# First four pairs of heads eased off ScalarE, two more parts of GEMM 2 in seven products, and a new instruction order

## The chip, the cores and the metric

The kernel runs on one core of one Trainium2 chip. The metric is the device time in microseconds, as a median of several runs. Beside it stands one execution taken by the hardware profiler. Engines are named as the profile names them: PE is TensorE, DVE VectorE, ACT ScalarE, POOL GpSimd, SP the engine that issues the DMAs.

## The reference

Attention with random features over 64 heads, and a two-layer network on its output:

```python
batch, n_heads, seq, head_dim = (8, 8, 576, 64); n_features = 128
n_tokens, d_model, d_ff = (4608, 512, 2048)
def phi(x):
    proj = np.einsum('bhsd,md->bhsm', x, omega)
    sq = np.sum(x * x, axis=-1, keepdims=True) / 2.0
    h = proj - sq
    h = h - np.max(h, axis=-1, keepdims=True)
    return np.exp(h) / np.sqrt(m)
q_p, k_p = (phi(q_s), phi(k_s))
kv = np.einsum('bhsm,bhsd->bhmd', k_p, v)
z = np.sum(k_p, axis=2)
num = np.einsum('bhsm,bhmd->bhsd', q_p, kv)
den = np.einsum('bhsm,bhm->bhs', q_p, z)[..., None] + 1e-06
...
h = x @ w_in
sp = np.maximum(h, 0.0) + np.log1p(np.exp(-np.abs(h)))
g = h * erf(sp)
return g @ w_out
```

All of it is float32.

## The kernel before

**Pairs.** Heads are done two at a time, 32 pairs, named `b_p` (batch and pair): `uk`, `uq` hold the transposed k and q of a pair with their squares, `ppk`, `ppq` the projections in PSUM, `mxk`, `mxq` the negated row maxima, `fk`, `fq` the exponentials, `kvp` and its copy `kh` the product of k's features with v, `pt` the transposed `fq`, `qh` its copy out of PSUM, `nd` numerator and denominator, `rc` the reciprocal by Ln and Exp on ACT, `xs` the quotient. The first eight pairs square with `square`, on 64 partitions; the first four are done before the network begins.

**Supers.** The network goes over six blocks of tokens ("supers") of 2 x 288, 2 x 288 and four times 2 x 432. A float32 product is made of three in fp32r, of a rounded part and a rest (`xh`, `xl`; `gh`, `gl`). GEMM 1 gives `h` (supers 0 and 1) or `hX`, `hY`, `hZ` (supers 2 to 5, where seven block products stand for eight; `PRODUCTS`). GEMM 2 goes in four parts (quarters of d_ff) per super. `FIRST2` says from which super a part has seven products (`gemm2_blocks`: banks `oX`, `oY`, `oZ`, operands `bb`, `bh`, `th`, `bl`, `tl` from `pieces2`) and not eight (`gemm2`: bank `o`, operands `gh`, `gl`). `pieces2` forms four differences (`gs`) and rounds five operands. The sums of weights that the seven products need are made by `make_sums` in the super ahead of the first that uses them, and stored in DRAM (`wdc`). Super 2's input needs the pairs up to 3_3.

**Weights.** Each block of weights comes as 64-bit words and is put together once: shift (`st`, DVE), a ScalarE step and a join (`wt`), a rounding and a rest (`w`), in supers 0 and 1.

**Order.** `build` lists operations with the engines that may take them, a cost and the slack from which an engine takes them. `Plan.order` plays them with estimated costs, `LAG` between engines, slots and due times; a program is emitted in the order that it picks, and each engine runs its own in that order. All compute instructions are issued on line 1008 (1031 in the changed kernel), so the names of tiles tell them apart.

Of the kernel before, what the change touches and what calls it, by code (L numbers as in the profile page):

```python
# [19 lines left out]
P = 128  # L20
# [44 lines left out]

FIRST2 = (3, 3, 3, 3)

# [7 lines left out]
BANDWIDTH = 270e3  # L75
LAG = {"T": 0.35, "A": 0.25, "V": 0.25, "G": 0.3, "S": 0.3}
SLOTS = dict(w=8, g=11, u=2, f=2, mx=3, sq=3, v=1, qh=1, ql=1, kh=1, kl=1, xs=12, xh=2, xl=2,
# [28 lines left out]
class Plan:  # L106
# [43 lines left out]
    def order(self, slots, caps):  # L150
# [167 lines left out]

AHEAD = 40.0

# [25 lines left out]
SQN = 4  # L346
SQG = -1e9
SQA = 4.0
# [4 lines left out]
def build(emit):  # L353
# [162 lines left out]
    def load(n, qk):  # L516
# [28 lines left out]
        for i in range(parts):  # L545
            keys = range(3) if parts == 1 else [i]
            f = 1.0 / parts
            pl.op("sq" + qk, [("A", 1.17 * f + .1, -1e9)] if n == 0 else
                  [("G", 2.2, SQG if n < SQN else -1e9), ("A", 1.2, -1e9 if n < SQN else SQA)],
                  lambda e, i=i: E.square(e, u, qk, i, parts),  # L550
                  reads=[(u, ("x", c)) for c in keys], writes=[(u, ("s", c)) for c in keys])

    def project(n, qk, t0):
# [15 lines left out]
        else:  # L569
# [5 lines left out]
            order = range(3)  # L575
        less = (n, qk) in LESS
        for i in order:
# [4 lines left out]
        if rows:  # L582
# [3 lines left out]
                  reads=keys + [(sq, 0)], writes=keys[:1] + [(mx, k) for k in range(NC)])  # L586
        for i in order:
            c = chunks[i]
            if less:
                pl.op("less" + qk, [("V", 0.56, -1e9)], lambda e, i=i, c=c: E.less(f, mx, banks[i], c),  # L590
                      reads=[(banks[i], 0)] + [(mx, k) for k in c], writes=[(f, k) for k in c])
# [4 lines left out]
        if less:  # L596
            pl.op("exp" + qk, [("A", 1.16, -1e9)], lambda e: E.exponential_all(f),
                  reads=[(f, k) for k in range(NC)], writes=[(f, k) for k in range(NC)], set="exp")

    def key_values(n, t0):  # L600
# [7 lines left out]
        kl = a["kl"] = kh if whole else pl.tile("kl", "kl" + a["nm"], [P, 2, P], F32R)  # L608
        pl.op("kvhigh", [("V", 0.6, -1e9), ("A", 0.7, -1e9)], lambda e: E.kv_high(e, kh, kvp),
              reads=[(kvp, 0)], writes=[(kh, 0)])  # L610
# [4 lines left out]
    def turn(n, t0):  # L615
# [48 lines left out]
    def split(b, c):  # L664
# [326 lines left out]
def tile_attention_moe(ctx: ExitStack, tc: tile.TileContext, qT, kT, qR, kR, qN, kN, vP, omT, w1, w2, out):  # L991
# [68 lines left out]
    class Emit:  # L1060
# [111 lines left out]

# [197 lines left out]
```

## Time and profile before

| | us |
|---|---|
| median of 3 runs (1030.12 to 1030.81) | 1030.14 |
| the profiled execution | 1036.67 |
| its span, first to last instruction | 1034.9 |
| PE busy in it | 1006.5 |
| DVE, ACT, POOL busy | 795.1, 683.7, 628.5 |
| mean granted clock of TensorE | 0.993 |

Busy time of PE counts pipelined products from start to modelled end, so a product's own cost is read from the distance of starts, or from a run of them in the chain of waits.

### The profile page before, as it was taken

What the parts mean: (1) busy time and instruction counts of PE and PEld (TensorE: products, weight loads), DVE (VectorE), ACT (ScalarE), POOL (GpSimd) and SP (SyncE); (2) the same over time, 40 slices, a digit from 0 to 9 for tenths busy, and PEclk for the clock granted to TensorE, in tenths of its full rate; (3) what the DMA queues carried; (4) which work ended last, traced back from release to release, by engine and by line L of the source; (5) the groups of instructions that cost most, each with busy time, mean ns of one, the idle gap of its engine ahead of it and who ended that gap; (6) DMA issues with size and microseconds to landing.
All of it is one profiled execution on the core that took longest, in us unless ns stands there. A gap on an engine that the chain in (4) does not pass through costs nothing.

```text
span 1034.9 us, 19457 instructions
## 1 busy us (share of the span) xinstructions
PE 1006.5 (97%) x7132; PEld 932.1 (90%) x7132; DVE 795.1 (77%) x1288; ACT 683.7 (66%) x1285; POOL 628.5 (61%) x467
## 2 busy tenths in 40 slices
PE   7999999999999899999999999999999999999998
PEld 6899889988999699999989899989899999999997
DVE  4888978897877747657787786889887788778664
ACT  7879887785676656855757575767658565645550
POOL 3435544875677728636876847569765388687520
PEclk9999998999999999999999999999999999999999
DMA  8276777597777467766547876666687546686651
GB/s 218 83 239 221 277 270 249 191 365 278 252 246 240 149 233 242 237 229 220 189 163 252 286 247 222 224 227 221 215 278 236 192 166 220 225 291 220 229 183 69
DMA packets 99486, 232.72 MB, mean 225 GB/s; under 512 B 11200, under 2 KB 11712, under 8 KB 99392
## 3 DMA queue, kind: packets, MB, share of 16 engines
q1 hardware_dynamic: 99232, 231.42, 67.1%
q8 instruction: 57, 0.93, 0.4%
q14 instruction: 37, 0.30, 0.1%
q10 hardware_dynamic: 160, 0.07, 0.0%
HBM read 188.45 MB, written 42.99 MB: 224 GB/s over the span
## 4 chain that ended last, share of the span: by engine, by line
PE 83%; DVE 8%; ACT 4%; DMA 3%; issue 2%; SPq 1%; ACTq 0%; DVEq 0%
PE o L1008 16%; PE hX L1008 14%; PE oX L1008 9%; PE h L1008 8%; PE hY L1008 7%; PE nd L1008 6%; PE oY L1008 5%; PE ppq L1008 4%; PE hZ L1008 4%; PE kvp L1008 3%; PE ppk L1008 3%; PE oZ L1008 2%; PE pt L1008 2%; DMA w<-wdw 1%; ACT L1008 1%
## 5 line engine op out<-in xcount | busy, mean ns | idle before, releaser
L1008 PE MATMUL o<-gh,w 128*128 128x288 f32 (+1 forms) x832 | 211.1, 329 | 0.6 <-DVE w L1008 0.6
L1008 PE MATMUL hX<-xh,wb 128*128 128x432 f32 x512 | 166.1, 370 | 2.3 <-DVE hs L1008 1.3
L1008 POOL TENSOR_TENSOR hs<-gs,hs 128x864 f32<-128x864 f32 (+1 forms) x44 | 97.6, 2242 | 101.0 <-ACT gs L1008 93.7
L1008 PEld LDWEIGHTS o<-gh,w 128*128 128x128 f32 x832 | 144.6, 188 | 6.1 <-DVE w L1008 1.1
L1008 PE MATMUL o<-gl,w 128*128 128x288 f32 (+1 forms) x416 | 132.7, 319 | 0.1
L1008 PE MATMUL h<-xh,w 128*128 128x288 f32 x512 | 126.0, 317 | 4.4 <-DVE w L1008 1.8
L1008 PEld LDWEIGHTS hX<-xh,wb 128*128 128x128 f32 x512 | 96.2, 188 | 9.1 <-DVE hs L1008 1.9
L1008 ACT ACT_TABLE_LOAD x75 | 96.2, 1283 | 2.1 <-PEq L1361 0.7
L1008 PEld LDWEIGHTS h<-xh,w 128*128 128x128 f32 x512 | 88.4, 193 | 9.4 <-DVE w L1008 2.5
L1008 PE MATMUL hX<-xl,wb 128*128 128x432 f32 x256 | 91.6, 358 | 0.0
L1008 ACT ACTIVATE fq<-ppq,mxq 128x128 f32<-128x128 f32 x288 | 78.6, 388 | 16.7 <-DVE mxq L1008 16.0
L1008 ACT ACTIVATE fk<-ppk,mxk 128x128 f32<-128x128 f32 x288 | 82.2, 380 | 9.7 <-DVE mxk L1008 9.3
L1008 ACT ACTIVATE hs<-hX 128x432 f32<-128x432 f32 x70 | 37.3, 532 | 74.6 <-PE hX L1008 73.8
L1008 PE MATMUL nd<-qh,kh 128*128 128x288 f32 x256 | 79.6, 417 | 7.2 <-ACT qh L1008 2.7
L1008 PE MATMUL hY<-xh,wb 128*128 128x432 f32 x256 | 84.0, 369 | 0.0
L1008 PE MATMUL oX<-th,wb 128*128 128x432 f32 x264 | 83.8, 367 | 0.0
L1008 ACT ACTIVATE rc<-nd,eps 64x288 f32<-64x288 f32 x128 | 63.6, 497 | 29.1 <-PE nd L1008 25.9
L1008 PEld LDWEIGHTS o<-gl,w 128*128 128x128 f32 x416 | 78.3, 188 | 2.9 <-DVE gl L1008 0.4
L1008 POOL TENSOR_TENSOR uq<-uq 128x288 f32<-128x288 f32 (+1 forms) x46 | 39.9, 888 | 67.2 <-PE h L1008 15.0
L1008 PE MATMUL h<-xl,w 128*128 128x288 f32 x256 | 76.7, 300 | 0.0
L1008 POOL TENSOR_TENSOR uk<-uk 128x288 f32<-128x288 f32 (+1 forms) x52 | 44.9, 884 | 51.1 <-DMA uk<-kT 23.4
L1008 DVE TENSOR_TENSOR xs<-nd,rc 64x288 f32<-64x288 f32 (+1 forms) x160 | 62.9, 393 | 14.9 <-ACT rc L1008 11.7
(142 smaller groups left out, 2700.2 us busy)
## 6 DMA issues: line engine op xcount, KB each, us to landing
wb<-wdc SPq DMA_DIRECT2D x216, 256.0 KB, 3.5
wb<-wdw SPq DMA_DIRECT2D x162, 256.0 KB, 3.8
w<-wdw SPq DMA_DIRECT2D x52, 512.0 KB, 4.5
st<-w SPq DMA_DIRECT2D x32, 512.0 KB, 5.0
wdw<-w SPq DMA_DIRECT2D x32, 512.0 KB, 4.4
wdc<-c SPq DMA_DIRECT2D x32, 512.0 KB, 4.8
v<-vP SPq DMA_DIRECT2D x32, 325.0 KB, 4.6
uk<-kR SPq DMA_DIRECT2D x24, 320.0 KB, 3.7
```

Of the source, the lines that this page charges most:

```text
L1008: return tc.keep_in_program_order(method(*args, **kwargs))
```

## The change

1. `FIRST2` goes from (3, 3, 3, 3) to (3, 3, 2, 2): parts 3 and 4 of GEMM 2 have seven products from super 2 on, and their sums of weights are made in super 1.
2. In the first pairs some steps may no longer go to ACT: pair 0's squares of q go to DVE, those of pairs 1 to 3 to POOL or DVE; the copies of `kvp` and `pt` of pairs 0 to 3 go to DVE alone; the rounding of super 0's input goes to POOL or DVE.
3. The planner's lags and `AHEAD` have other values, and `JITTER` moves due times within 26 stretches by fixed amounts, so that the order differs almost everywhere.
4. The three projections into a bank now have one start and one stop flag. `LIFT` and `LESS` are empty lists: the code that they switch emits nothing.

```diff
-FIRST2 = (3, 3, 3, 3)
+FIRST2 = (3, 3, 2, 2)
-LAG = {"T": 0.35, "A": 0.25, "V": 0.25, "G": 0.3, "S": 0.3}
+LAG = {"T": 0.32375, "A": 0.2525, "V": 0.2605, "G": 0.2979, "S": 0.2925}
+        for k, (lo, hi, amp) in enumerate(JITTER):
+            for o in ops:
+                if lo <= o.due < hi:
+                    o.due += amp * ((o.id * 7919 + k * 104729 + 17) % 1009 / 504.0 - 1.0)
-AHEAD = 40.0
+JITTER = ((0, 0, 0), (186.1, 206.1, 4), (0, 0, 0), (0, 0, 0), (0, 0, 0), (227.5, 727.5, 4),
...
+AHEAD = 39.82
-SQG = -1e9
+SQV = 3.0
+EASED = 4
-            pl.op("sq" + qk, [("A", 1.17 * f + .1, -1e9)] if n == 0 else
-                  [("G", 2.2, SQG if n < SQN else -1e9), ("A", 1.2, -1e9 if n < SQN else SQA)],
+            pl.op("sq" + qk, [("A" if qk == "k" else "V", 1.17 * f + .1, -1e9)] if n == 0 else
+                  [("G", 2.2, -1e9), ("V", 1.27, SQV)] if n < SQN else [("G", 2.2, -1e9), ("A", 1.2, SQA)],
-        pl.op("kvhigh", [("V", 0.6, -1e9), ("A", 0.7, -1e9)], lambda e: E.kv_high(e, kh, kvp),
+        pl.op("kvhigh", [("V", 0.6, -1e9), ("A", 0.7, -1e9)][:1 + (n >= EASED)], lambda e: E.kv_high(e, kh, kvp),
-            pl.op("turnhigh", [("A", 0.5, -1e9), ("V", 0.5, -1e9)],
+            pl.op("turnhigh", [("V", 0.5, -1e9), ("A", 0.5, -1e9)][:1 + (n >= EASED)],
-            pl.op("xhigh", [("A", 0.2 + 0.24 * m, -1e9), ("G", 0.1 + 0.35 * m, 2.0),
-                            ("V", 0.1 + 0.18 * m, -1e9)],
+            pl.op("xhigh", [("A", 0.2 + 0.24 * m, -1e9)] * (b > 0) +
+                  [("G", 0.1 + 0.35 * m, 2.0), ("V", 0.1 + 0.18 * m, -1e9)],
+            elif e == "V":
+                dve.tensor_mul(u.ap[dst, c], u.ap[src, c], u.ap[src, c])
-                          rhs=wq if qk == "q" else wk, start=True, stop=True)
+                          rhs=wq if qk == "q" else wk, start=c == 0, stop=c == 2)
```

Three places show what that does to the order.

ACT at the start of the program, before (`uk`, `uq` are squares, `fk`, `fq` exponentials; the last number of a name only counts tiles):

```order
L1008 ACTIVATE uk_0_0_84<-uk_0_0_84 64x384 x3
L1008 ACTIVATE uq_0_0_88<-uq_0_0_88 64x384 x2
L1008 ACTIVATE fk_0_0_124<-ppk_0_0_0_96,mxk_0_0_107 128x128 x3
L1008 ACTIVATE fk_0_0_124<-ppk_0_0_1_103,mxk_0_0_107 128x128 x3
L1008 ACTIVATE fk_0_0_124<-ppk_0_0_2_112,mxk_0_0_107 128x128 x3
L1008 ACTIVATE uq_0_0_88<-uq_0_0_88 64x384
L1008 ACTIVATE fq_0_0_154<-ppq_0_0_0_120,mxq_0_0_137 128x128 x3
L1008 ACTIVATE fq_0_0_154<-ppq_0_0_1_131,mxq_0_0_137 128x128 x3
L1008 ACTIVATE fq_0_0_154<-ppq_0_0_2_158,mxq_0_0_137 128x128 x3
L1008 ACTIVATE uk_0_2_128<-uk_0_2_128 64x1152
L1008 ACTIVATE fk_0_1_222<-ppk_0_1_0_192,mxk_0_1_205 128x128 x3
L1008 ACTIVATE qh_0_0_237<-pt_0_0_1_226 128x384
```

and DVE at the start of the changed program:

```order
L1031 TENSOR_REDUCE mxk_0_0_103<-ppk_0_0_0_96 128x3
L1031 TENSOR_TENSOR uq_0_0_88<-uq_0_0_88 64x384 x2
L1031 TENSOR_REDUCE mxk_0_0_103<-ppk_0_0_1_107 128x3
L1031 TENSOR_REDUCE mxk_0_0_103<-ppk_0_0_2_118 128x3
L1031 TENSOR_TENSOR uq_0_0_88<-uq_0_0_88 64x384
L1031 TENSOR_REDUCE mxq_0_0_146<-ppq_0_0_0_126 128x3
L1031 TENSOR_REDUCE mxq_0_0_146<-ppq_0_0_1_134 128x3
L1031 TENSOR_REDUCE mxq_0_0_146<-ppq_0_0_2_148 128x3
L1031 TENSOR_TENSOR uq_0_1_105<-uq_0_1_105 64x1152
L1031 COPY kh_0_0_194<-kvp_0_0_165 128x2x64
L1031 COPY kh_0_0_194<-kvp_0_0_165 128x128
L1031 TENSOR_REDUCE mxk_0_1_204<-ppk_0_1_0_188 128x3
```

The squares of q of pairs 0 and 1 stand on DVE now; pair 2's k is squared on POOL, and all three copies `qh` of pair 0 follow on DVE.

PE where super 2 begins, before (`hX2` is its first GEMM 1 bank, `nd_3_3` pair 3_3):

```order
L1008 MATMUL hX2_0_1_4602<-xh2_0_4335,wb63_4345 128x432
L1008 MATMUL pt_3_3_2_4673<-ident_67,fq_3_3_4583 128x128 x3
L1008 MATMUL nd_3_3_0_0_4682<-qh_3_3_4636,kh_3_3_4592 128x288
L1008 MATMUL nd_3_3_1_0_4686<-qh_3_3_4636,kh_3_3_4592 128x288
L1008 MATMUL nd_3_3_0_1_4690<-qh_3_3_4636,kh_3_3_4592 128x288
L1008 MATMUL nd_3_3_1_1_4701<-qh_3_3_4636,kh_3_3_4592 128x288
L1008 MATMUL ppq_4_0_0_4707<-wr_71,uq_4_0_4570 128x128
```

and the same four nd in the changed program, 42 products `o1`, nine of `ppq_4_0` and a `kvp` ahead of its first `hX2`:

```order
L1031 MATMUL nd_3_3_1_0_4536<-qh_3_3_4438,kh_3_3_4360 128x288
L1031 MATMUL o1_2_2_0_4518<-gh1_5_4150,w2_1_2_0_58_4105 128x288
L1031 MATMUL o1_2_2_0_4518<-gl1_5_4224,w2_1_2_0_58_4105 128x288
L1031 MATMUL o1_2_2_0_4518<-gh1_5_4150,w2_1_2_0_58_4105 128x288
L1031 MATMUL nd_3_3_0_1_4545<-qh_3_3_4438,kh_3_3_4360 128x288
L1031 MATMUL o1_2_2_0_4518<-gh1_5_4150,w2_1_2_0_58_4105 128x288
L1031 MATMUL o1_2_2_0_4518<-gl1_5_4224,w2_1_2_0_58_4105 128x288
L1031 MATMUL o1_2_2_0_4518<-gh1_5_4150,w2_1_2_0_58_4105 128x288
L1031 MATMUL o1_2_1_0_4550<-gh1_4_4143,w2_1_1_0_59_4174 128x288
L1031 MATMUL o1_2_1_0_4550<-gl1_4_4177,w2_1_1_0_59_4174 128x288
L1031 MATMUL o1_2_1_0_4550<-gh1_4_4143,w2_1_1_0_59_4174 128x288
L1031 MATMUL nd_3_3_1_1_4558<-qh_3_3_4438,kh_3_3_4360 128x288
```

They have moved from behind super 2's first products to between the last of super 1.

PE in part 3 of GEMM 2 of super 2, before and now (the third number of `o2_2_0_0` is its output block; `bb` is block B11 rounded and its rest, so three rows read alike):

```order
L1008 MATMUL o2_2_0_0_6198<-gh2_4_5911,w2_1_0_0_101_6046 128x432
L1008 MATMUL o2_2_0_0_6198<-gl2_4_5940,w2_1_0_0_101_6046 128x432
L1008 MATMUL o2_2_0_0_6198<-gh2_4_5911,w2_1_0_0_101_6046 128x432
L1008 MATMUL nd_4_3_0_0_6205<-qh_4_3_6151,kh_4_3_5990 128x288
L1008 MATMUL nd_4_3_1_0_6215<-qh_4_3_6151,kh_4_3_5990 128x288
```

```order
L1031 MATMUL oX2_2_0_6260<-bb2_2_6108,wb101_6099 128x432 x3
L1031 MATMUL pt_4_3_2_6270<-ident_67,fq_4_3_6035 128x128 x3
L1031 MATMUL oX2_2_1_6274<-bb2_2_6108,wb101_6099 128x432 x6
L1031 MATMUL oX2_2_0_6260<-bb2_2_6108,wb101_6099 128x432 x3
L1031 MATMUL nd_4_3_0_0_6296<-qh_4_3_6225,kh_4_3_6003 128x288
```

Parts 3 and 4 together have 192 such products in the order before and 168 in the new one.

## Rows read from the trace of the kernel before

**Rows 1.** The page: busy us, share of the span and instructions of each engine; and the granted clock of TensorE in 40 slices, in tenths.

```profile
PE 1006.5 (97%) x7132; PEld 932.1 (90%) x7132; DVE 795.1 (77%) x1288; ACT 683.7 (66%) x1285; POOL 628.5 (61%) x467
...
PEclk9999998999999999999999999999999999999999
```

**Rows 2.** The chain of waits in order of time: start, us, what.

```profile
507.05 14.35 PE o L1008 x72
```

**Rows 3.** Windows of 40 us: busy us (and instructions) of each engine, granted clock, DMA share, GB/s.

```profile
400.00:440.00 40.00, 40.00 (x271) 37.06 (x267) 28.00 (x45) 28.54 (x56) 27.72 (x23) 1.00 0.71 236
440.00:480.00 40.00, 40.00 (x257) 36.92 (x256) 26.65 (x48) 24.45 (x41) 19.65 (x17) 1.00 0.66 219
480.00:520.00 40.00, 40.00 (x227) 37.23 (x226) 29.92 (x45) 25.02 (x39) 29.65 (x20) 1.00 0.59 195
520.00:560.00 40.00, 38.65 (x292) 34.70 (x291) 30.87 (x55) 24.97 (x55) 25.56 (x21) 1.00 0.65 218
```

The columns after the length are PE, PEld, DVE, ACT and POOL.

**Rows 4.** Timeline of PE, the first 50 us: start, us, instruction, and in brackets the idle time before it with what ended it.

```profile
10.22 0.94 PE L1008 MATMUL ppq<-wqk,uq 128*128 128x128 f32 x6 [0.69 <-ACT uq L1008]
...
18.46 3.25 PE L1008 MATMUL nd<-qh,kh 128*128 128x288 f32 x6 [1.93 <-ACT qh L1008]
...
28.44 2.25 PE L1008 MATMUL nd<-qh,kh 128*128 128x288 f32 x8
...
37.33 2.25 PE L1008 MATMUL nd<-qh,kh 128*128 128x288 f32 x8
...
47.23 0.75 PE L1008 MATMUL nd<-qh,kh 128*128 128x288 f32 x2 [1.16 <-DVE qh L1008]
```

**Rows 5.** Timeline of PE where super 2 begins.

```profile
346.64 0.47 PE L1008 MATMUL hX<-xh,wb 128*128 128x432 f32 x1 [0.76 <-ACT fq L1008]
...
352.88 1.80 PE L1008 MATMUL nd<-qh,kh 128*128 128x288 f32 x6 [0.52 <-ACT fk L1008]
355.92 0.75 PE L1008 MATMUL nd<-qh,kh 128*128 128x288 f32 x2 [1.24 <-DVE xs L1008]
...
360.02 0.80 PE L1008 MATMUL ppq<-wr,uq 128*128 128x128 f32 x2 [2.26 <-DVE xs L1008]
...
363.73 0.46 PE L1008 MATMUL hZ<-xh,wb 128*128 128x432 f32 x1 [0.55 <-ACT kh L1008]
```

**Rows 6.** Windows of 5 us, columns as in rows 3 (the clock is the third number from the end).

```profile
15.00:20.00 5.00, 2.94 (x11) 1.88 (x10) 2.04 (x4) 3.87 (x10) 2.65 (x3) 0.84 1.03 301
20.00:25.00 5.00, 5.00 (x58) 4.37 (x56) 2.42 (x6) 4.25 (x13) 2.25 (x2) 0.82 1.03 260
155.00:160.00 5.00, 4.67 (x18) 4.32 (x19) 4.58 (x9) 3.64 (x8) 3.57 (x4) 0.50 0.94 339
360.00:365.00 5.00, 4.43 (x44) 3.99 (x45) 2.50 (x6) 2.93 (x9) 3.76 (x2) 0.69 0.53 146
```

**Rows 7.** Groups of instructions, shapes kept apart: out<-in, count, busy us, mean ns of one, idle before.

```profile
L1008 POOL TENSOR_TENSOR tl<-gs,th 128x864 fp32r<-128x864 f32 x24 | 58.5, 2459 | 5.7 <-DVE bl L1008 2.9 <-DVE th L1008 2.1 <-ACT th L1008 0.5
...
L1008 DVE TENSOR_TENSOR xs<-nd,rc 64x288 f32<-64x288 f32 x96 | 43.5, 453 | 13.2 <-ACT rc L1008 11.2
...
L1008 DVE TENSOR_TENSOR os<-oX,os 128x432 f32<-128x432 f32 x70 | 41.4, 603 | 17.9 <-PE oX L1008 17.5
...
L1008 POOL TENSOR_TENSOR gs<-hs,gs 128x432 f32<-128x432 f32 x22 | 35.0, 1614 | 2.0 <-DVE gs L1008 2.0
...
L1008 DVE TENSOR_TENSOR tl<-gs,th 128x1728 fp32r<-128x1728 f32 x10 | 23.3, 2331 | 2.8 <-POOL tl L1008 2.3 <-POOL th L1008 0.4
...
L1008 ACT ACTIVATE th<-gs 128x1728 fp32r<-128x1728 f32 x14 | 23.2, 1657 | 18.3 <-DVE gs L1008 7.0 <-POOL gs L1008 4.7 <-PE o L1008 3.7
...
L1008 DVE TENSOR_TENSOR gs<-hs,gs 128x864 f32<-128x864 f32 x11 | 19.8, 1801 | 1.8 <-POOL gs L1008 1.0 <-POOL hs L1008 0.8
L1008 DVE TENSOR_TENSOR xs<-nd,rc 64x144 f32<-64x144 f32 x64 | 19.5, 304 | 1.6 <-ACT rc L1008 0.5
```

**Rows 8.** Timeline of ACT, the first 20 us.

```profile
5.39 0.99 ACT L1008 ACTIVATE uq<-uq 64x384 f32<-64x384 f32 x2
...
15.97 1.16 ACT L1008 ACTIVATE uk<-uk 64x1152 f32<-64x1152 f32 x1 [3.30 <-DMA uk<-kT]
...
17.91 0.50 ACT L1008 ACTIVATE qh<-pt 128x384 f32<-128x384 f32 x1
```

**Rows 9.** Timeline of POOL, the first 60 us.

```profile
10.82 2.25 POOL L1008 TENSOR_TENSOR uk<-uk 64x576 f32<-64x576 f32 x2 [9.51 <-DMA uk<-kT]
13.15 2.25 POOL L1008 TENSOR_TENSOR uq<-uq 64x576 f32<-64x576 f32 x2
...
49.77 2.25 POOL L1008 TENSOR_TENSOR uk<-uk 64x576 f32<-64x576 f32 x2 [3.58 <-DMA uk<-kT]
```

**Rows 10.** Timeline of DVE, the first 60 us.

```profile
13.36 1.90 DVE L1008 TENSOR_REDUCE mxk<-ppk 128x3 f32<-128x384 f32 x3 [0.37 <-PE ppk L1008]
15.18 1.06 DVE L1008 COPY qh<-pt 128x384 f32<-128x384 f32 x2
...
44.85 0.47 DVE L1008 CAST xh<-xs 128x288 fp32r<-128x288 f32 x1
...
48.03 0.68 DVE L1008 SCALAR_TENSOR_TENSOR wt<-wt,st 128x512 int32<-128x512 int32 x1
...
51.05 1.14 DVE L1008 CAST xh<-xs 128x288 fp32r<-128x288 f32 x1
```

More of the change, by code (lines that the diff above doesn't have):

```diff
@@ L326 @@
 WHOLE2 = (0, 0)
+LIFT = []
 LESS = []
@@ L575, in project @@
             order = range(3)
-        less = (n, qk) in LESS
         for i in order:
@@ L586, in project @@
                   reads=keys + [(sq, 0)], writes=keys[:1] + [(mx, k) for k in range(NC)])
-        for i in order:
+        lift, less = (n, qk) in LIFT, (n, qk) in LESS
+        for i in order if lift or less else ():
             c = chunks[i]
-            if less:
-                pl.op("less" + qk, [("V", 0.56, -1e9)], lambda e, i=i, c=c: E.less(f, mx, banks[i], c),
-                      reads=[(banks[i], 0)] + [(mx, k) for k in c], writes=[(f, k) for k in c])
+            if lift:
+                pl.op("lift", [("T", len(c) * COST["proj"], -1e9)],
+                      lambda e, i=i, c=c: E.lift(banks[i], mx, c),
+                      reads=[(mx, k) for k in c] + [(banks[i], 0)], writes=[(banks[i], 0)])
+            else:
+                pl.op("less" + qk, [("V", 0.15 + 0.135 * len(c), -1e9)], lambda e, i=i, c=c: E.less(f, mx, banks[i], c),
+                      reads=[(banks[i], 0)] + [(mx, k) for k in c], writes=[(f, k) for k in c])
+        if less:
+            pl.op("exp" + qk, [("A", 1.16, -1e9)], lambda e: E.exponential_all(f, f.ap, range(NC)),
+                  reads=[(f, k) for k in range(NC)], writes=[(f, k) for k in range(NC)], set="exp")
+        for i in () if less else order:
+            c = chunks[i]
+            if lift:
+                pl.op("exp" + qk, [("A", 0.2 + 0.107 * len(c), -1e9)],
+                      lambda e, i=i, c=c: E.exponential_all(f, E.chunks(banks[i], c), c),
+                      reads=[(banks[i], 0)], writes=[(f, k) for k in c], set="exp")
                 continue
@@ L595, in project @@
                   reads=[(banks[i], 0)] + [(mx, k) for k in c], writes=[(f, k) for k in c], set="exp")
-        if less:
-            pl.op("exp" + qk, [("A", 1.16, -1e9)], lambda e: E.exponential_all(f),
-                  reads=[(f, k) for k in range(NC)], writes=[(f, k) for k in range(NC)], set="exp")
     def key_values(n, t0):
@@ L1163, in shift, with lift, chunks, exponential_all @@
                 dve.scalar_tensor_tensor(dst, sq.ap, x, raw, op0=ALU.mult, op1=ALU.add)
+        def lift(self, b, mx, c):
+            for i, k in enumerate(c):
+                pe.matmul(b.ap[:, i * P:(i + 1) * P], lhsT=ident, rhs=mx.ap[:, k:k + 1].broadcast_to([P, P]),
+                          start=False, stop=True, skip_group_check=True)
         def less(self, f, mx, b, c):
             n = len(c)
-            dve.tensor_add(f.ap[:, c[0]:c[0] + n, :], b.ap[:, :n * P].rearrange("p (c m) -> p c m", c=n),
+            dve.tensor_add(f.ap[:, c[0]:c[0] + n, :], self.chunks(b, c),
                            mx.ap[:, c[0]:c[0] + n].rearrange("p (c m) -> p c m", m=1).broadcast_to([P, n, P]))
-        def exponential_all(self, f):
-            act.activation(f.ap, f.ap, AF.Exp)
+        def chunks(self, b, c):
+            return b.ap[:, :len(c) * P].rearrange("p (c m) -> p c m", c=len(c))
+        def exponential_all(self, f, src, c):
+            act.activation(f.ap[:, c[0]:c[0] + len(c), :], src, AF.Exp)
         def exponential(self, f, mx, b, c):
```

6 rows, old and new, of the table JITTER are left out of this document.

## The prediction

> **What bounds the kernel now.** I read the page first: TensorE is busy 97% of the span and its clock stands at full speed in all but a slice or two [rows 1]. So only three things can change the time: the number of TensorE instructions, the few places where TensorE waits, and the stretches where it runs at the lower of its two clock levels. From the chain of waits I took what one product costs while nothing is late: 72 of 432 columns in 14.35 us, 0.199 us each [rows 2]. The stage windows over 400 to 560 us show how full the other engines are where the change adds work to them: DVE 115.4, ACT 103.0 and POOL 102.6 us of 160, while TensorE idles only 1.35 us [rows 3]. The timelines then show the places where TensorE does wait. The first 50 us (four pairs of heads, with no products of super 0 yet to fill gaps) have waits of 0.69, 1.93 and 1.16 us [rows 4]. The start of super 2, 346 to 364 us, has five waits in a row [rows 5]. The windows say what a cluster of waits costs besides: after them the granted clock reads 0.84 and 0.82 (15 to 25 us), 0.50 (155 to 160 us) and 0.69 (360 to 365 us) [rows 6].
>
> The sum is made against the profiled execution (span 1034.9, 1036.67 us with what lies around it). That execution is 6.5 us longer than the median of the runs shown, 1030.14; I take differences from the trace and put them, one for one, on the median.
>
> **Seven products in two more parts.** Parts 3 and 4 of GEMM 2 in super 2 go from 96 to 84 products each (192 and 168 TensorE instructions for both in the two orders), so 24 products of 432 columns go: 24 x 0.199 = **-4.7 us** [rows 2]. All of it is on the bounding engine. What it adds lies on the others, per part: four differences of 864 columns (1.80 on DVE), roundings and rests of one and a half granules more (1.5 x 1.66 on ACT and 1.5 x 2.33 on DVE), six additions more into the output (0.60): 7.2 + 2.5 + 3.5 + 3.6 = 16.8 us, 34 for two [rows 7]. The idle time of the three engines in 400 to 560 us is 44.6 + 57.0 + 57.4 = 159 us [rows 3], which hides it unless it falls on one engine at one time; that case is a rival. Weight sums of these parts are made one super earlier, an equal amount of work moved, not added.
>
> **The first four pairs.** ACT gives up the squares of pair 0's q (0.99 us for two, then a third) and of pair 2's k, which sat at 15.97 behind a transfer and held pair 1's exponentials and the copy of pair 0's qh (17.91 us) behind it [rows 8]. For that copy TensorE waited 1.93 us before 18.46 [rows 4]. In the new order DVE makes all three copies of qh; ahead of them stand now the square of pair 1's q and a third copy. No row shows this square on DVE. The products of xs bound it: 453 ns for 288 columns and 304 ns for 144 [rows 7] make 1.03 ns a column and 155 ns fixed, so 0.55 us for 384 columns and 1.35 us for 1152. POOL took the same square at 13.15, with no wait, after pair 1's k, which came at 10.82 [rows 9], so its data landed between these two times. If it lands by 11.8 us the square is over before pair 1's maxima at 13.36 and qh is ready at 15.18 + 3 x 0.53 = 16.8 [rows 10]; if at 13.1, it ends at 14.45, the copies of kh and the three maxima behind it (1.90 us for the maxima with their waits [rows 10], some 2 us for both back to back) end about 1.2 us later than they did, and qh comes at about 18.0. Against the 18.46 of the row that is a gain between 0.4 and 1.7 us; I take 1.0, the data landing midway. TensorE's 0.69 us for the third square of q goes too, but what follows waits for the same maxima, so it is not counted twice.
>
> From pair 1 to pair 2 TensorE works without a gap (nd at 28.44 and again at 37.33, 8.9 us for a pair, no idle time noted [rows 4]): easing ACT gains nothing there. The wait of 1.16 us at 47.23 is for a DVE copy of qh and stays, since DVE only gets more to do. Two things are left: the low clock of 15 to 25 us costs 0.16 x 5 + 0.18 x 5 = 1.7 us [rows 6], of which I give back half, since the wait in front of it is halved, and the first weights are joined on DVE between pairs 1 and 2 instead of after pair 3, worth some 0.7 us, one of the three steps that stood there from 48.03 on [rows 10] with TensorE's first products behind them. Sum: -1.0 - 0.8 - 0.7 = **-2.5 us**, from +1 (the square late, the copies late) to -5 (all waits and the low clock gone).
>
> **Pair 3_3 ahead of super 2.** In the old order the four nd of pair 3_3, the last that super 2's input needs, come after super 2 has begun, with nothing behind them but work that depends on them. TensorE waits 0.76, 0.52, 1.24, 2.26 and 0.55 us [rows 5], 5.3 in all, and 360 to 365 us runs at 0.69 of the clock: 0.31 x 5 = 1.5 us [rows 6]. Together 6.9. In the new order these four stand among products of GEMM 2 of super 1, and from the last of them to super 2's first product there are 42 products of 288 columns (about 0.13 us each by their pitch, two thirds of the 0.199 [rows 2]), a projection and a kvp: some 8 us of work. The old chain from the nd at 355.92 to the first hZ of super 2 took 7.8 us [rows 5]; so it fits, barely. Bounds: 0 (the waits move along) and -6.9. I take **-6.0 us**.
>
> **What it gives back.** Attention done earlier in super 1 and 30 us more on POOL, ACT and DVE are new chances for a late operand. The one price that a row offers for a single such wait in a full stage is the 1.35 us of 520 to 560 us [rows 3]; I put **+1.5 us**. Other waits move, too; from rows I can't say which way, so they count 0, with 4 us either side in the range. The flags of the projections, the empty lists (LIFT, LESS) and AHEAD change no instruction that waits. Sum: -4.7 - 2.5 - 6.0 + 1.5 = -11.7, so **1018.4 us**.
>
> **The shared port.** A cast on DVE took 0.47 us at 44.85 and 1.14 us at 51.05 [rows 10], the second within a POOL product that ran from 49.77 to 52.02 [rows 9]. The Trainium skill, GPSIMD Engine Reference, section Key points, says that GpSimd shares its SBUF interfaces with VectorE and contends with DVE instructions that have two SBUF inputs, which speaks against squares on DVE beside squares on POOL; this row agrees in kind, though its cast has one input. As a mechanism of this kernel: pair 1's square on DVE stands beside POOL's two halves, 2.25 us for both [rows 9], and is held for one of them, 1.1 us; the 1.0 us gained at 18.46 is lost and the time is 1019.4.
>
> **The rivals.**
> - *The forecast*: products, head and pair 3_3 as summed, 1014 to 1022. Chance 0.45.
> - *Held by POOL in the head*, 1019.4, as above. Chance 0.08. It hardly differs in time; the trace would show it.
> - *The waits of pair 3_3 only move.* The attention of pairs 2_3 to 4_0 stands earlier, in super 1, and if the ACT and DVE steps behind their products are as late there, the 6.0 comes back: 1024.4. For it: the chain fits by only 0.3 us; against: products of super 1 stand between. Chance 0.17.
> - *Slower: several moved pairs wait.* The same steps, but with at least three of the moved pairs late as pair 3_3 was, 6.9 us each: 3 x 6.9 = 20.7, less the 5.7 net of the other terms and the 6.9 that goes: 1030.1 - 5.7 - 6.9 + 20.7 = 1038. It is slower than before from 12.6 us of new waits, two such pairs. Against it: in 400 to 560 us the same pairs are done beside products with one wait of 1.35 us [rows 3]. Chance 0.04.
> - *POOL is late with the new parts.* From the third part of super 2 through the first of super 3 the order gives POOL six more halves tl (2.46 each) and twelve more halves gs (1.6 each), 34 us, less what it sheds there, about 10 [rows 7]; of 480 to 560 us it has 25 idle [rows 3]. Each of four leases of operands then waits as 520 to 560 us shows, 1.35: +5.4, 1023.8. Chance 0.12.
> - *More waits go.* TensorE stands still for 28.4 us of the span [rows 1]; without the start, the end and the waits named above some 11 are left. If a third of that goes, and the low clock at 155 to 160 us (0.50, 2.5 us [rows 6]) with it, some 6 us more: 1012. Chance 0.12.
> - *It doesn't do what it says*: the orders show that it does; 0.02, within 0.2% of before.
>
> **How the numbers follow.** The likeliest case gives 1018.4. The range 1011 to 1027 takes in the forecast, the port, the moved waits, POOL and nearly all of the better case, and leaves out less than 0.2. Two microseconds, 0.2%, are about what a measurement of this kernel can tell from no change. Faster by more than that (below 1028.1): all but the last of the moved waits, the slower case and the empty one, 0.91; within 0.2%: 0.05; slower: 0.04.
>
> **What would show it.** Right: 24 fewer products of 432 columns; nd of pair 0 without a wait near 2 us for qh; no five waits at the start of super 2, and the granted clock there at 1.00; TensorE busy 97% or more. Wrong: waits for qh, fq or xs between 240 and 330 us; waits of oY or oX for POOL's tl or gs between 490 and 600 us; the square of pair 1's q on DVE starting after 13 us; waits of h for w longer than before up to 160 us.

## The result, and the profile after

| | median, us | runs | range, us |
|---|---|---|---|
| before | 1030.81 | 9 | 1030.12 to 1033.20 |
| changed | 1037.04 | 9 | 1034.96 to 1047.31 |

The ratio is 1.0073, 95% interval 1.0046 to 1.0100. The change makes the kernel slower by 0.7%; the forecast was 1018.4 us, a gain. The profiled execution of the changed kernel took 1038.60 us.

The page of the changed kernel: busy times, granted clock, and the shares of the chain that ended last.

```profile
PE 1003.3 (97%) x7108; PEld 927.9 (89%) x7108; DVE 818.4 (79%) x1302; ACT 699.5 (67%) x1303; POOL 639.1 (62%) x471
...
PEclk9999999998999999999999999999999999999999
...
PE 73%; DVE 10%; POOL 6%; ACT 4%; issue 3%; DMA 3%; SPq 1%; POOLq 0%; DVEq 0%; ACTq 0%
```

The 24 products are gone (7132 instructions before, [rows 1]) and the start of super 2 is clean: from 340 to 380 us TensorE has no wait that the timeline notes. POOL holds 6% of the chain that ended last, and had no share of it before:

```profile
PE 83%; DVE 8%; ACT 4%; DMA 3%; issue 2%; SPq 1%; ACTq 0%; DVEq 0%
```

Timeline of PE in the changed kernel, the larger waits (columns as in [rows 4, 5]):

```profile
16.35 0.75 PE L1031 MATMUL nd<-qh,kh 128*128 128x288 f32 x2 [1.21 <-DVE qh L1031]
...
31.98 1.37 PE L1031 MATMUL kvp<-v,fk 128*64 128x130 f32 x36 [1.68 <-DVE w L1031]
37.70 0.75 PE L1031 MATMUL nd<-qh,kh 128*128 128x288 f32 x2 [1.00 <-DVE qh L1031]
...
119.09 0.37 PE L1031 MATMUL h<-xh,w 128*128 128x288 f32 x1 [2.27 <-DVE w L1031]
...
236.93 1.33 PE L1031 MATMUL nd<-qh,kh 128*128 128x288 f32 x2 [2.15 <-ACT qh L1031]
...
526.09 0.55 PE L1031 MATMUL pt<-ident,fq 128*128 128x128 f32 x3 [2.06 <-DVE os L1031]
...
811.60 0.47 PE L1031 MATMUL hX<-xh,wb 128*128 128x432 f32 x1 [2.49 <-ACT hs L1031]
...
898.81 0.46 PE L1031 MATMUL oX<-th,wb 128*128 128x432 f32 x1 [1.43 <-DVE os L1031]
```

Windows of the changed kernel, columns as in [rows 6]:

```profile
20.00:25.00 5.00, 5.00 (x70) 4.81 (x69) 4.46 (x11) 4.65 (x17) 3.08 (x4) 1.00 1.02 232
120.00:125.00 5.00, 5.00 (x24) 4.41 (x25) 4.87 (x8) 2.50 (x9) 3.49 (x4) 0.69 0.86 315
...
235.00:240.00 5.00, 3.07 (x10) 2.65 (x11) 4.60 (x7) 4.24 (x13) 5.00 (x4) 0.57 0.81 273
...
360.00:365.00 5.00, 5.00 (x27) 4.79 (x26) 5.00 (x7) 1.94 (x3) 5.00 (x4) 1.00 0.60 205
810.00:815.00 5.00, 3.40 (x13) 3.22 (x14) 3.76 (x6) 1.54 (x2) 0.00 (x0) 0.76 0.31 107
```

The low clock left 20 to 25 and 360 to 365 us and now stands behind the new waits at 119, 237 and 811.

To compare whole stages I charged each product with the usual pitch of its form, that is of its tile and shape (its mean distance to the next start in a second execution of before, where no pitch counts for more than 60 ns over the form's median). What TensorE's time exceeds that is lost, to waits and to the low clock alike. Stages are cut by work done, not by time, so that they hold the same products; a column is named by its end (-200 is 120 to 200). Lost us:

```
work done, us            0-60 60-120 -200 -240 -300 -320 -460 -560 -740 -end   sum   work
before  (1036.67 us)     14.4    3.6 10.2  3.6  2.6  9.3  3.5  5.9  8.9 -0.2  61.8  964.8
before  (1030.55 us)     10.2    3.6  9.2  3.7  2.6  8.3  3.5  5.9  9.1 -0.2  55.8  964.8
changed (1038.60 us)     15.4    5.7  8.1  8.6  2.7  0.5  3.5  9.1  9.3  6.3  69.0  959.9
changed (1036.89 us)     12.9    5.5  9.5  7.8  2.8  0.5  3.5  9.2  9.3  6.2  67.2  959.9
mended  (1022.78 us)     11.3    3.5  6.6  4.9  3.6  0.5  3.5  8.0  9.3  2.0  53.2  959.9
```

The work falls by 4.9 and the start of super 2 (column -320) by 7.8 to 8.8, as forecast in kind and place. The stages to 120, to 240, to 560 and from 740 on lose about 16 us more: that is the result. The second rows and the last are of the experiments.

### The profile page after: what moved, and what is told of

Read it like the earlier page. It is cut to its first block, busy times and chain, and to the rows that moved or that the text cites. A ratio compares the mean times of both kernels' runs of the same rounds, so it can differ in the third digit from the quotient of the medians.

```text
span 1036.8 us, 19457 instructions
## 1 busy us (share of the span) xinstructions
PE 1003.3 (97%) x7108; PEld 927.9 (89%) x7108; DVE 818.4 (79%) x1302; ACT 699.5 (67%) x1303; POOL 639.1 (62%) x471
## 4 chain that ended last, share of the span: by engine, by line
PE 73%; DVE 10%; POOL 6%; ACT 4%; issue 3%; DMA 3%; SPq 1%; POOLq 0%; DVEq 0%; ACTq 0%
PE o L1031 12%; PE hX L1031 12%; PE h L1031 10%; PE oX L1031 9%; PE hY L1031 6%; PE nd L1031 5%; PE oY L1031 4%; PE ppq L1031 3%; PE hZ L1031 3%; PE ppk L1031 3%; PE kvp L1031 3%; PE pt L1031 2%; POOL hs L1031 2%; PE oZ L1031 2%; DMA st<-w 1%
## 5 line engine op out<-in xcount | busy, mean ns | idle before, releaser
L1031 POOL TENSOR_TENSOR hs<-gs,hs 128x864 f32<-128x864 f32 (+1 forms) x54 | 110.2, 2065 | 111.4 <-ACT gs L1031 95.5
L1031 PE MATMUL hX<-xh,wb 128*128 128x432 f32 x512 | 170.1, 370 | 4.0 <-ACT hs L1031 3.6
L1031 PE MATMUL o<-gh,w 128*128 128x288 f32 (+1 forms) x704 | 169.7, 319 | 0.0
L1031 PEld LDWEIGHTS o<-gh,w 128*128 128x128 f32 x704 | 120.7, 188 | 3.2
L1031 PE MATMUL o<-gl,w 128*128 128x288 f32 (+1 forms) x352 | 110.0, 312 | 0.7 <-DVE gl L1031 0.7
L1031 PE MATMUL oX<-th,wb 128*128 128x432 f32 x312 | 102.1, 368 | 1.6 <-DVE os L1031 1.6
L1031 PE MATMUL hY<-xh,wb 128*128 128x432 f32 x256 | 87.1, 371 | 0.0
L1031 POOL TENSOR_TENSOR uq<-uq 128x288 f32<-128x288 f32 (+1 forms) x46 | 47.1, 1044 | 51.7 <-DMA uq<-qN 20.9
L1031 DVE TENSOR_TENSOR os<-oX,os 128x432 f32<-128x432 f32 x86 | 50.9, 603 | 23.7 <-PE oX L1031 23.4
L1031 ACT ACTIVATE gs<-hs 128x1728 f32<-128x1728 f32 (+1 forms) x48 | 69.4, 1481 | 0.3
```

The lines of the kernel that those rows point to most:

```text
L1031: return tc.keep_in_program_order(method(*args, **kwargs))
```

## The experiments

In the expectations, theory Q says that the new waits come from the order in the engines' queues: an instruction that waits for a late engine stands ahead of the one that TensorE needs. Rival W says that the engines have more work there than they can do, so that a wait only moves. Theory P came last: POOL's running instruction holds DVE back.

**Both kernels once more**, unchanged.

> The kernel before, unchanged, profiled once more. Theory 1 (the base of the sum was wrong): the profile that the prediction was read from ran 1036.67 us, some 6 us over the ordinary 1030 to 1033, and the 6.9 us of waits and low clock at the start of super 2 are what it has more. Then an execution near 1030 to 1032 shows no row of waits of 0.5 to 2.3 us between 340 and 365 us, and the granted clock stays near 1.00 there. Theory 2 (the waits are a part of the order, the 6 us are the profiler's): the same five waits stand there, 5 us or more in sum.

> The changed kernel, unchanged, profiled once more. If its new waits (2.2 us before 119.1, 2.1 before 236.9, 2.1 before 526.1, 2.5 before 811.6, 1.4 before 898.8 us) belong to the order, at least four of the five stand there again within 1 us of their size. If they come and go between executions, most are gone or elsewhere, and the time differs from 1038.6 by over 2 us.

Before took 1030.55 us. Its timeline of PE at super 2:

```profile
341.41 0.47 PE L1008 MATMUL hX<-xh,wb 128*128 128x432 f32 x1 [0.76 <-ACT fq L1008]
...
350.68 0.75 PE L1008 MATMUL nd<-qh,kh 128*128 128x288 f32 x2 [1.23 <-DVE xs L1008]
354.78 0.49 PE L1008 MATMUL ppq<-wr,uq 128*128 128x128 f32 x2 [2.26 <-DVE xs L1008]
```

and its windows:

```profile
15.00:20.00 5.00, 4.87 (x33) 3.91 (x33) 2.81 (x7) 4.87 (x15) 2.43 (x2) 1.00 1.04 304
20.00:25.00 5.00, 4.87 (x65) 4.42 (x65) 4.84 (x13) 4.24 (x16) 2.71 (x3) 1.00 1.06 258
...
355.00:360.00 5.00, 4.38 (x54) 3.69 (x54) 2.86 (x7) 3.79 (x12) 4.00 (x3) 1.00 0.70 196
```

The waits of super 2 are there to 0.01 us: they belong to the order. Of the 6.0 us that the profiled execution lost more, 4.2 were in the head: the 1.93 us at 18.46 [rows 4] and the low clock of 15 to 25 us [rows 6] are gone here (table: 14.4 against 10.2). Another 1.0 each stand in the columns -200 and -320: the low clock behind super 2's waits is gone too (1.00 here, 0.69 in [rows 6]), and that near 155 us is shorter. So theory 1 held for the head and for the low clock, not for the waits. The changed kernel took 1036.89 us; all five of its waits stand again, four within 0.03 us of their size and that at 237 us with 1.57 for 2.15, so they too belong to the order.

**The seven products alone, and the changed work in an order not picked.**

```diff
-FIRST2 = (3, 3, 3, 3)
+FIRST2 = (3, 3, 2, 2)
```

> The kernel before with FIRST2 = (3, 3, 2, 2) alone, its order played anew. If 24 products of 432 columns are worth 4.7 us and the added work is hidden: 1026 us, with no wait over 0.5 us in 480 to 600 us that before does not have. If the added work of DVE, ACT and POOL is what makes the changed kernel slow: 1032 us or more, with waits of oX or oY for operands or for banks.

Measured 1035.63, ratio 1.0041 (1.0026 to 1.0055). Its profile loses 65.9: 13.1 at the start of super 2 (four more than before), 9.4 in the stage to 560.

```diff
-LAG = {"T": 0.32375, "A": 0.2525, "V": 0.2605, "G": 0.2979, "S": 0.2925}
+LAG = {"T": 0.35, "A": 0.25, "V": 0.25, "G": 0.3, "S": 0.3}
-AHEAD = 39.82
+AHEAD = 40.0
+JITTER = ()
```

> The changed kernel with LAG and AHEAD of before and an empty JITTER: both edits of the work, the order not replayed by other numbers. If the order is what costs: 1024 to 1030 us. If the work of the first pairs and of the new parts costs: 1035 us or more, as the changed kernel.

Measured 1040.28, ratio 1.0087 (1.0069 to 1.0105): slower than the changed kernel, and lost at other places, 23.9 us in the stage to 740. So the order picked is some 3 us better than the unpicked one; the waits are not tied to the places of the added work. By their expectations both runs came out on the side of the added work: neither is near the 1026, or the 1024 to 1030 us, of its other case. They can't tell whether the work costs by itself or through the orders that the planner makes of it; the kernel mended below, with all the work, decides that.

**The order alone, and another order of the same kind.** First the kernel before with only LAG, AHEAD and JITTER of the changed one; then the changed one with `o.id * 7907` for `o.id * 7919` in JITTER.

> The kernel before with no change of its work, its order played with LAG, AHEAD and JITTER of the changed kernel. If a newly played order costs by itself, whatever the work: 1033 to 1040 us, with waits of 1 to 4 us at places where before has none. If the new numbers are good and the added work is what costs: 1028 us or less.

Measured 1034.02 (1024.74 to 1037.70 in 12 runs). The median lies in the first range and its profile has a wait of 2.56 us before 623.27 where before has none, but before took 1032.11 beside it, and the ratio is 0.9998 (0.9972 to 1.0024): the new numbers deal the waits anew, and cost nothing that can be measured without the changed work.

> The changed kernel with another multiplier in JITTER's hash (7907 for 7919): the same work and the same planner, another order that nobody picked. If an order's waits are dealt anew with each change of it, and the picked one is better than most: 1037 to 1046 us, with waits of 1 to 4 us at places that the changed kernel does not have. If the waits come from the work, they stand at the same places (112 to 119, 231 to 237, 526, 811, 898) and the time is 1035 to 1039.

Measured 1045.72, ratio 1.0123 (1.0101 to 1.0145). Its largest waits:

```profile
362.54 2.43 PE L1031 MATMUL kvp<-v,fk 128*64 128x130 f32 x36 [3.90 <-DVE hs L1031]
...
683.38 0.46 PE L1031 MATMUL hY<-xh,wb 128*128 128x432 f32 x1 [2.41 <-DVE os L1031]
```

None stands at 526, 811 or 898. The 2.27 us before `h` do stand again, at 115 us; JITTER moves no due time between 47.8 and 186.1 us. Three orders that the planner made of the same work (this, the unpicked, the changed) span 1037.0 to 1045.7 us, and with the one mended by hand below 1023.5 to 1045.7: the order, with the choice of engines that goes with it, decides over some 22 us, the products over 4.9.

**Three repairs by hand.** The order stays; a few operations are moved in the list from which each engine's program is emitted. `(x, "after", y)` puts operation x right behind y.

```diff
-    for o in plan.order(slots, CAPS):
+    for o in moved(plan.order(slots, CAPS)):
+MOVES = [(3926, "after", 4058), (4262, "after", 4430), (4270, "after", 4262), (2618, "after", 2693),
+         (2608, "after", 2618), (2610, "after", 2608), (2609, "after", 2610)]
```

Here a rounding `th` goes behind the copy of `hX4_1_1` (ACT), a difference `gs` and its `th` behind an addition to the output (DVE, ACT), and sums and maxima of pair 5_1 behind another (DVE).

> The changed kernel in its own order, with seven instructions moved on ACT and DVE where TensorE waited at 526.1 (2.1 us), 811.6 (2.5) and 898.8 (1.4): each time the instruction that TensorE waits for now stands ahead of one that waits for another engine. Theory Q (the new waits come from an instruction that stands in an engine's queue behind one that is late): the three waits fall under 0.4 us, the low clock after 811.6 goes with its wait, and the time falls by 6 to 8 us, to 1029 to 1031. Rival W (the engines have more work there than they can do, so a wait only moves): the three places lose as much within 15 us behind, and the time falls by less than 2.5 us.

Measured 1033.94, ratio 1.0011 (0.9982 to 1.0039), about 3 us less than the changed kernel, between the two cases. The wait at 899 is gone (that stage's excess is 1.6 smaller), that of 526 fell to half, and that of 811 only moved (DVE and PE in its profile):

```profile
807.78 1.96 DVE L1045 TENSOR_TENSOR tl<-gs,th 128x1728 fp32r<-128x1728 f32 x1 [0.61 <-ACT th L1045]
809.65 0.60 DVE L1045 TENSOR_TENSOR hs<-hZ,hs 128x432 f32<-128x432 f32 x1
810.17 0.60 DVE L1045 TENSOR_TENSOR hs<-hX,hs 128x432 f32<-128x432 f32 x1
810.31 0.90 PE L1045 MATMUL pt<-ident,fq 128*128 128x128 f32 x3 [2.60 <-DVE hs L1045]
```

TensorE went on for 2.2 us more of its work and then waited for the next queue: DVE's additions of hZ and hX stand behind a `tl` that waits for the `th` moved back. For this place W was right so far.

```diff
+MOVES = [(1110, "after", 1135), (1111, "after", 1110), (1136, "after", 1148), (460, "after", 601),
+         (461, "after", 460), (597, "before", 585), (599, "before", 587)]
```

> The same with seven instructions moved at 106 to 120 us and at 222 to 237 us: two roundings of g on DVE (and the rests on POOL behind them), which wait for POOL's gates, go behind the maxima and the joins of weights that TensorE waits for; a block of weights that is wanted first is joined first; a copy of qh goes ahead of an exponential. Theory Q: of 3.9 us of waits at 114.7 to 119.1 some 1.5 are left, of 4.2 at 232.5 to 236.9 some 2; 4 to 6 us less, 1031 to 1033. Rival W: less than 1.5 us.

Measured 1031.05, ratio 0.9997 (0.9973 to 1.0022): some 6 us less, as theory Q said. Lost to 120: 4.0 for 5.5; to 240: 4.8 for 7.8.

```diff
+ENGINE = [(46, "G"), (138, "A")]
+MOVES = [(138, "after", 137), (131, "after", 142), (134, "after", 131)]
```

> The changed kernel with the square of pair 1's q back on POOL, one copy of pair 2's qh back on ACT, and a maximum of pair 3 behind the copies. If the easing of ACT put the wait on DVE (the square took 1.92 us there, the three copies stand behind three maxima): the waits of 0.7 to 1.2 us before pair 0's and of 1.0 before pair 2's numerators fall under 0.4 us each, 1.5 to 2.5 us less. If the head is bound by its transfers: no change within 0.5 us.

Measured 1037.28, ratio 1.0045 (1.0016 to 1.0074): against the changed kernel no difference that these runs show. In the profile the wait before pair 0's numerators fell under 0.4 us, that of pair 2 moved to its second product, and the head lost 11.9 us for 12.9 to 15.4. What the square of pair 1's q does there shows in the changed kernel's second execution (POOL, DVE, PE of the first pairs):

```profile
9.53 2.25 POOL L1031 TENSOR_TENSOR uk<-uk 64x576 f32<-64x576 f32 x2 [8.22 <-DMA uk<-kT]
...
11.07 1.92 DVE L1031 TENSOR_TENSOR uq<-uq 64x1152 f32<-64x1152 f32 x1 [0.27 <-DMA uq<-qT]
...
14.80 1.48 DVE L1031 COPY qh<-pt 128x384 f32<-128x384 f32 x3
15.41 0.75 PE L1031 MATMUL nd<-qh,kh 128*128 128x288 f32 x2 [0.71 <-DVE qh L1031]
```

The square on DVE began 0.27 us after DVE was free, took 1.92 us and ended 1.2 us behind POOL's squares, which ended at 11.78.

**The shift of a weight that waits for its transfer.**

```diff
+MOVES = [(239, "before", 227)]
```

> The changed kernel with one instruction moved: DVE's shift of the second block of weights, which waits for its transfer (0.4 to 3.2 us in the traces so far) between pairs 1 and 2, goes behind pair 2's copies of qh. If that transfer, late in some executions, is what spreads the head: no wait for a weight on DVE before 35 us, TensorE's 1.85 us before 31.98 gone where it stood, 0.5 to 2 us less on the median, 1035 to 1036.5. If the head is late by its other transfers: within 0.5 us of the changed kernel.

The row of DVE that it is about, in the profile of the changed kernel:

```profile
30.17 0.43 DVE L1031 TENSOR_SCALAR st<-st 128x512 int32<-128x512 int32 x1 [2.93 <-DMA st<-w]
```

Measured 1035.28, ratio 1.0045 (1.0024 to 1.0065), and no wait before `kvp` near 32 us. The gain of 1.8 us on the median is of the expected size, but inside the spread, and the changed kernel's second execution waits only 0.23 us there without the move. Of its twelve executions nine took 1033.5 to 1035.6 us and three 1043.9 to 1044.3; the profile is of one of the three, and shows what they have more. The timelines of PE, of DVE and of POOL at the start of super 3, one after the other:

```profile
523.69 0.70 PE L1045 MATMUL hX<-xh,wb 128*128 128x432 f32 x1 [10.80 <-issue]
```

```profile
508.58 14.62 DVE L1045 TENSOR_TENSOR xl<-xs,xh 128x432 fp32r<-128x432 f32 x1
523.12 0.47 DVE L1045 COPY kh<-kvp 128x128 f32<-128x128 f32 x2
```

```profile
508.20 3.30 POOL L1045 TENSOR_TENSOR xl<-xs,xh 128x432 fp32r<-128x432 f32 x3
511.43 4.03 POOL L1045 TENSOR_TENSOR hs<-gs,hs 128x864 f32<-128x864 f32 x2
515.38 1.33 POOL L1045 TENSOR_TENSOR uq<-uq 128x288 f32<-128x288 f32 x2
516.62 2.18 POOL L1045 TENSOR_TENSOR gs<-hs 128x432 f32<-128x432 f32 x2
518.72 4.00 POOL L1045 TENSOR_TENSOR hs<-gs,hs 128x864 f32<-128x864 f32 x2
522.82 1.87 POOL L1045 TENSOR_SCALAR bh<-hs 128x1728 fp32r<-128x1728 f32 x1
```

A subtraction that takes DVE 1.20 us in the profile of the changed kernel took 14.62, while POOL ran one instruction after the other without a gap, and ended 0.5 us after the last of that chain (522.72). TensorE stood for 10.80 us.

Shorter holds of this kind, past the end of the POOL instruction that ran when DVE's began, stand in the profiles of other runs too. In that of the order alone (DVE and POOL) one ends just before the copies of hX, and those end the wait before 623.27:

```profile
614.99 7.20 DVE L1019 TENSOR_TENSOR bb<-hs,bb 128x864 fp32r<-128x864 f32 x1
622.11 1.11 DVE L1019 COPY hs<-hX 128x432 f32<-128x432 f32 x2
615.05 2.20 POOL L1019 TENSOR_TENSOR gs<-hs,hs 128x432 f32<-128x432 f32 x2
617.19 4.08 POOL L1019 TENSOR_TENSOR bl<-hs,bh 128x864 fp32r<-128x864 f32 x2
```

The shortest time of that `bb` in any profile is 1.04 us. The seven products alone have one of 6.14 us for 1.94 at 538, the other seed one of 4.48 for 1.04 at 673, before its wait at 683.

**POOL's instruction taken away.** That opened theory P. At 811 us the changed kernel shows (POOL, DVE, ACT):

```profile
801.92 5.71 POOL L1031 TENSOR_TENSOR bl<-hs,bh 128x864 fp32r<-128x864 f32 x2
...
802.80 2.90 DVE L1031 TENSOR_TENSOR gs<-hs,gs 128x864 f32<-128x864 f32 x1
...
805.63 3.82 DVE L1031 TENSOR_TENSOR tl<-gs,th 128x1728 fp32r<-128x1728 f32 x1
...
809.48 1.64 ACT L1031 ACTIVATE th<-gs 128x1728 fp32r<-128x1728 f32 x1 [5.52 <-DVE tl L1031]
...
811.03 0.51 ACT L1031 ACTIVATE hs<-hX 128x432 f32<-128x432 f32 x1
```

The copy of hX that TensorE waits for stands behind the `th`, that behind DVE's `tl`, and DVE behind POOL.

```diff
+ENGINE = [(3921, "V")]
+MOVES = [(3921, "after", 3925)]
```

> The changed kernel with one instruction given to another engine: the rest bl of part 2 of super 4, two POOL instructions of 2.85 us from 801.9 on, is done by DVE behind its first tl. In the trace two DVE instructions end 1.1 and 2.0 us after the ends of these two, as if each had waited for POOL's running one. Theory P (POOL's instruction holds DVE's back, and that makes the wait at 811.6): without it DVE's gs takes 1.1 to 1.8 us for 2.9 and its tl 2.0 to 2.4 for 3.8, although DVE now has 2 us more to do, TensorE's 2.5 us before 811.6 falls under 0.5 and 3 to 5 us less are lost from 800 to 820, low clock included. Theory Q alone (the queue of ACT is at fault, POOL has no part): DVE's two instructions take as long as before, and the wait stays at 2 us or grows.

DVE with POOL's work added:

```profile
800.40 1.04 DVE L1045 TENSOR_TENSOR gs<-hs,gs 128x864 f32<-128x864 f32 x1
801.37 1.94 DVE L1045 TENSOR_TENSOR tl<-gs,th 128x1728 fp32r<-128x1728 f32 x1
803.25 1.94 DVE L1045 TENSOR_TENSOR bl<-hs,bh 128x1728 fp32r<-128x1728 f32 x1
```

Three instructions took 4.9 us where two had taken 6.7. The wait at 811 is gone, and the last stage loses 2.4 us for 6.2. That is theory P, with no queue of ACT changed. The median is 1035.17, ratio 1.0041 (1.0015 to 1.0068): 2 us less than the changed kernel, within the spread of both, and five of twelve executions took over 1039 us. Even the profiled one, of 1032.27 us, has a longer hold: an `xl` at 498 us took 6.88 us for 1.94, and TensorE waits 1.92 us before 505.

**All repairs.** First the three repairs together, with more moves (DVE's `tl` at 811 behind the additions too, the maxima at 526 further back, the blocks of weights that are wanted first joined first):

```diff
+ENGINE = [(46, "G"), (138, "A")]
+MOVES = [(3926, "after", 4058), (3927, "after", 4074), (4262, "after", 4430), (4270, "after", 4262),
+         (2618, "after", 2696), (2608, "after", 2618), (2610, "after", 2608), (2609, "after", 2610),
+         (2611, "after", 2609), (2612, "after", 2611),
...
+         (597, "after", 598), (472, "after", 597), (599, "after", 597), (600, "after", 599), (601, "after", 600), (460, "before", 492),
...
+         (781, "after", 793), (780, "after", 792), (650, "after", 777), (653, "after", 650),
...
```

> The changed kernel in its own order with all the moves of the three kernels before, and four places mended further: at 811.6 us the rest tl, on which DVE's additions of hZ and hX waited in turn, goes behind them too; at 526 the rest of the maxima goes behind the additions to the output; at 106 to 120 the first block of weights is joined ahead of the exponentials; at 150 to 160 the block wanted first has its shift first. Theory Q (order in the queues): the lost time of the changed kernel falls by 4 at 811, 2 at 526, 1.5 at 899, 3 to 4 at 112 to 120, 3 at 232 to 238, 1 to 2 at 149 to 160: 14 to 16 us in sum, 1021 to 1025 us, faster than both kernels. Rival W (the engines have too much work there): 1028 or more, with new waits of over 1 us within 15 us of each place.

Measured 1028.74, ratio 0.9940 (0.9915 to 0.9964): faster than before, but not by what was expected. Its profile has new waits of 1.81 us before 521 and 2.14 before 574. That the second form of the moves at 526 made both is not shown: just ahead of the second DVE's rounding `th` was held 4.65 us for 1.05, through two POOL instructions. With the moves in their first form, and the shift moved:

```diff
-         (2618, "after", 2696), (2608, "after", 2618), (2610, "after", 2608), (2609, "after", 2610),
-         (2611, "after", 2609), (2612, "after", 2611),
+         (2618, "after", 2693), (2608, "after", 2618), (2610, "after", 2608), (2609, "after", 2610),
+         (239, "before", 227),
```

> All the moves of the kernel mended at all places, with this shift moved too, and the moves at 526 us taken back to their first form (the second made new waits of 2.0 us at 521 and 2.3 at 574). Theory Q: 3 to 5 us less than the kernel mended at all places, 1023 to 1026 us, 0.993 of before or less. Rival W: the waits at 521 and 574 come back elsewhere, 1028 or more.

Measured 1023.53 (1022.78 to 1024.89 in 5 runs), ratio 0.9919 (0.9907 to 0.9931): faster than both kernels, as theory Q said, with all the work of the changed one (one square and one copy of the first pairs stand on POOL and ACT again). Its page:

```profile
PE 997.1 (98%) x7108; PEld 923.1 (90%) x7108; DVE 813.9 (80%) x1300; ACT 700.3 (69%) x1304; POOL 644.9 (63%) x473
```

## Why the prediction was wrong, by its own steps

- *Seven products, -4.7*: right. The work fell by 4.9, and the mended kernel shows that the engines can hide the added work. What the forecast's 34 us of added work leaves out is DVE's waiting for POOL. I took, for every DVE instruction that reads only SBUF (TENSOR_REDUCE aside), the shortest time of its form in any profile: what they took beyond it is 94 to 96 us before and 109 in the changed kernel. So some 14 of the 23 us by which DVE's busy time grew are waiting. The mended kernel has 107: where it falls matters, not its sum.
- *Pair 3_3, -6.0*: right in mechanism and place, sized too small by 2: 8.3 to 9.3 us lost there became 0.5, outside the bounds of 0 and -6.9. Of the 6.9, the 1.5 for the low clock stood on one execution; the second has the same waits at full clock and loses 8.3 all the same, so the 5.3 us of waits that the rows note were the part sized too small. The rival that these waits only move did not come.
- *The first four pairs, -2.5*: wrong. The 1.93 us and the low clock, 1.8 of the 2.5, were taken from one execution that had them of its own; the second shows neither. The 0.7 for the first weights joined earlier has the other sign in some executions: DVE then waits up to 2.9 us for their transfer between pairs 1 and 2. And the square took 1.92 us where 1.35 was the bound; that DVE waited for POOL's squares is read from its end behind them, for this square ran alone in no profile. The head loses 1 to 3 us more.
- *What it gives back, +1.5*: **the step that failed.** In place of 1.5 stand +2.0 (to 120), +4.6 (to 240), +3.3 (to 560) and +6.5 (from 740): 16 us, by the means of the two executions of each. I priced one wait of a full stage, as if a newly played order kept the good places of the old one. That other waits "count 0, with 4 us either side" held the same error: the three orders that the planner made of this work lie over 8.7 us, and over 22 with the mended one.
- *The base*: differences of a profile 6 us over the median were put on the median one for one, though the prediction named the gap; of its 6, 4.2 us were the head's and 1.0 each lay at 155 and 360 us.
- *The rivals*: POOL holding the square in the head was right as a mechanism, and too narrow: the same hold costs far behind too, at 811 us. POOL late with the new parts was priced at +5.4 for 480 to 560 us; that stage lost 3.3. Several moved pairs waiting, the slower rival, is not what came: pairs 2_3 to 4_0 do not wait as pair 3_3 did. But the pair just ahead of them, 2_2, does: its numerators wait 0.80 and 2.15 us before 234.0 and 236.93.

What is shown: moving instructions in the queues, two of them to another engine, with all work kept, takes 13.5 us off the changed kernel; at 811 us POOL's instruction is the first cause. Argued only: that the waits at 112 to 119 and 231 to 237 also begin with DVE held by POOL. There a rounding that waits for POOL's gates stands ahead in DVE's queue, which order alone explains:

```profile
112.35 1.96 DVE L1031 CAST gh<-hs 128x1152 fp32r<-128x1152 f32 x1 [2.31 <-POOL hs L1031]
```

Open: which part of the spread of the changed kernel (two of nine runs over 1046 us) is the long hold seen at 508 us; those two runs have no trace. Not tried: the mended order with the products of before, so how much of the 13.5 us the same moves would take off the kernel before is open too.

## What to carry to other kernels

A change that replays the order of a full kernel is priced by what orders differ in, not by the one wait that can be seen to go; take that spread from two or three other orders before counting on 5 us (8.7 us here, for three). Read two executions before pricing a wait: those that stand in both to 0.01 us belong to the order; of the others, those before 18.46 and 31.98 us hung on a transfer. When TensorE waits, follow the chain of queues to its first late instruction and move what is needed past it; if a DVE instruction there is longer than its kind, look at POOL first.

## What the runs showed of the hardware

A DVE instruction that reads only SBUF and begins while a POOL instruction runs ends, nearly always, its own time after the end of that one: 2.90 us for 1.04, 3.82 for 1.94 at 802 to 809 us. In the changed kernel's second execution 153 of 155 such instructions (two-input ones, casts and shifts) end within 0.2 us of POOL's end plus the shortest time of their form in any profile. None of the 26 TENSOR_REDUCE over SBUF and of the 594 instructions with an operand in PSUM that began so took over 0.03 us more than the shortest of its form. The shift of 128x512 words has a median of 0.42 us over the 16 that ran wholly outside POOL's instructions and 1.34 over the 8 wholly inside its unbroken work, while additions from PSUM (`oX`) show 0.607 and 0.602. The hold need not end with one POOL instruction: 14.62 us through a gapless chain, for 1.20 in another execution, and shorter cases up to 7.20 for 1.04 in other runs.

The Trainium skill, GPSIMD Engine Reference, section Key points, names as contending the DVE instructions in a two-port mode or with two SBUF inputs, and Trainium Architecture — The Big Picture, section 🎯 What this means for kernel authors, calls it an exclusive lock and not a split of bandwidth. The rows agree with both: what reads PSUM is not held, and a held instruction ends its own time after POOL's, rather than running slower in proportion. The shifts and casts have one SBUF input, and no run here shows in which mode they ran.
